# The written order of an attention and token-mixing kernel: later loads, stores and the steps behind the first scores rearranged

## Chip, cores and metric

The kernel runs on one core of one Trainium2 chip. The metric is device time in microseconds (us) of one execution. Five engines with a queue each take part: PE (matrix products; its weight loads are shown as PEld), DVE and ACT (elementwise work, and the only two that read PE's results here), POOL (elementwise work in on-chip memory, and the issue of DMAs that convert float32 to bfloat16) and SP (the issue of DMAs).

## The reference, cut to what matters

Per batch and head, 32 learned tokens p attend over the sequence, and the sequence then attends over the 32 packed tokens. A mixing layer over the tokens and an output projection follow.

```python
p_packed = sm_attn(p, k, v)              # scale, softmax over 576 keys
out = sm_attn(q, p_packed, p_packed)     # softmax over 32 packed tokens
x = out.transpose(0, 2, 1, 3).reshape(B, S, H * D)      # 8 x 576 x 512
wq, wk = x @ w_q, x @ w_k                               # 512 -> 64
mixed = einsum('bst,btd->bsd', scale * wq @ wk^T, x)
result = maximum(mixed, 0) @ w_out                      # 8 x 576 x 512
```

There are 8 batches, 8 heads, 576 positions and a head size of 64; q, k, v and the result are float32 in HBM.

## The kernel before, in words

The work is cut by batch (b = 0 to 7) and, within a batch, into steps. One string, ORDER (L12 to L57), lists some 520 items; the loop at L599 emits them one after the other, and each engine executes its own items strictly in that order. `@A`, `@V`, `@P`, `@S` name the engine (ACT, DVE, POOL, SP) where there is a choice, and `=4,5` names the PSUM banks (eight banks hold PE's results until an engine has copied them out). Nothing else decides the order: an item that waits holds back everything behind it on its engine, and nothing on the others.

The items of a batch, in the order of their data:

- **Loads.** LD.k, LD.v, LD.q (L154 to L182) are issued by POOL; LD.v is two DMAs, LD.q7 and LD.r7 are the two halves of batch 7's q, LD.O is the output weight `wout`. There are four buffers of each kind (NL, L8).
- **First attention.** KT (L255) transposes k on DVE; S1 (L263) makes the scores on PE; X1 (L287) their exponentials on ACT; TE (L295) transposes them on DVE; PV (L306) multiplies by v on PE, with a column of ones for the sum; RC and PP (L318, L321) divide, PT (L326) transposes, both on DVE. QK (L331) multiplies the packed tokens by w_k and w_q; QKE (L341) copies the result out of PSUM, and QD (L344) copies part of it on POOL.
- **Second attention.** QV (L351) transposes q on DVE; S2 (L362) makes scores on PE; X2 (L375) exponentials on ACT; RS and RR (L390, L396) row sums and reciprocals on DVE (HA, L385, adds halves on POOL first for batch 5); AM (L401) multiplies on POOL; AT (L409) transposes on PE and AE (L421) copies out. The last number is the piece of the sequence (TCH, L359): 0 and 1 are 256 rows each, 2 the last rows, 3 is 0 and 1 together, 4 all.
- **Mixing.** WKQ and WE (L433, L456), GM and GE (L461, L470), Y and YE (L473, L481): PE, then a copy. MX and MR (L488, L494) make the mixed rows, RL, RLF and RLR (L515 to L524) apply the maximum with 0.
- **Output.** OT (L527) and OH (L574) multiply by `wout`, four matmuls for 128 rows; OE, OEF and OEH (L545, L548, L580) copy the result out, ST, STF and STH (L555, L588, L583) store it. OT.b.4 covers the remaining rows of two batches; OEF.b.4 copies them to a tile `orem` of which there are two (L550), so that OEF.5.4 writes what ST.1.4 (L557 to L559) stores from, and OEF.7.4 what ST.3.4 stores from. The tile `o` has six buffers (NO).
- **WARM** (L610) are matmuls on a constant tile whose result nobody reads; WARM.6 covers 6 x 128 columns.

HOLD.v7 (L567) is a tiny DMA on SP that reads v7's buffer: it is issued once v7 has landed, and SP's stores stand behind it.

Of the kernel before, what the change touches and what calls it, by code (L numbers as in the profile page):

```python
# [17 lines left out]
AM.0.2@P WARM.6=7 AT.0.2=7 AE.0.2@A RS.0.0@V RR.0.0@V KT.1.2@V WARM.5=6 S1.1=2,3,0,1 X1.1.0@A AM.0.0@P
RS.0.1@V AT.0.0=6 RR.0.1@V AE.0.0@V TE.1.0@V QD.0@P WARM.2=4 WKQ.0.0=4,5 WKQ.0.2 X1.1.1@A TE.1.1@V AM.0.1@P
AT.0.1=7 LD.q2 PV.1.0=2,3 PV.1.1 WE.0.0@V RC.1@V AE.0.1@A WKQ.0.1 WE.0.1@A WARM.2=6 GM.0=6 LD.k3 PP.1.1@V  # L20
PP.1.0@V PT.1@V QV.1.2@V GE.0@A WARM.1=0 Y.0=0,1 YE.0@A QK.1=4 QKE.1@V WARM.1=7 S2.1.2=2,3 S2.1.1=6,7 X2.1.2@A
RS.1.2@V S2.1.0=0,1 X2.1.1@A LD.O MR.0=4,5 RR.1.2@V AM.1.2@P RLR.0@A KT.2.2@V MX.0.1=2,3 WARM.3=6 AT.1.2=6
X2.1.0@A QD.1@P WARM.1=7 S1.2=4,5,0,1 RL.0.1@A LD.v3 AE.1.2@A MX.0.0=2,3 X1.2.1@A RS.1.0@V RR.1.0@V RS.1.1@V
AM.1.0@P X1.2.0@A TE.2.1@V RR.1.1@V AM.1.1@P TE.2.0@V RL.0.0@A WARM.6=7 AT.1.0=7 AE.1.0@V PV.2.0=0,1 PV.2.1
LD.k4 RC.2@V PP.2.0@V AT.1.1=6 AE.1.1@A LD.q3 LD.v4 WKQ.1.0=4,5 WKQ.1.2 WE.1.0@A PP.2.1@V WKQ.1.1 WE.1.1@A
PT.2@V QK.2=2 QKE.2@A QV.2.2@V LD.q4 WARM.1=3 GM.1=3 QD.2@P GE.1@A WARM.1=7 Y.1=6,7 S2.2.2=0,1 X2.2.2@A
KT.3.2@V S2.2.3=4,5 YE.1@A WARM.1=2 MX.1.0=2,3 X2.2.3@A MX.1.1=0,1 MR.1=6,7 RLR.1@A RS.2.4@V RL.1.0@A RR.2.4@V
# [1 line left out]
AM.2.3@P OT.0.3 OT.0.0=4,5 AT.2.3=2 TE.3.0@V PV.3.0=0,1 PV.3.1 OE.0.1@V LD.k5 OT.0.1 RC.3@V PP.3.1@V PP.3.0@V
AE.2.3@A LD.v5 WKQ.2.0=6,7 WKQ.2.1 LD.k6 OE.0.0@A PT.3@V LD.q5 WKQ.2.2 KT.4.2@V QK.3=3 WE.2.2@A QKE.3@A  # L30
OT.1.0=0,1 S1.4=4,5,6,7 X1.4.1@A QV.3.2@V GM.2=2 GE.2@A OT.1.1 OE.1.0@V X1.4.0@A TE.4.0@V Y.2=6,7 YE.2@A
S2.3.2=2,3 X2.3.2@A S2.3.3=4,5 MX.2.1=6,7 MX.2.0=2,3 OT.1.2=0,1 TE.4.1@V X2.3.3@A QD.3@P OT.1.3 RS.3.4@V
MR.2=4,5 RR.3.4@V AM.3.3@P AM.3.2@P RL.2.1@A RLR.2@V LD.v6 PV.4.0=6,7 RL.2.0@A PV.4.1 LD.q6 RC.4@V PP.4.1@V
OE.1.1@A PP.4.0@V PT.4@V OT.2.2=2,3 QK.4=4 QV.4.2@V AT.3.3=5 QKE.4@A AT.3.2=4 AE.3.2@A S2.4.2=0,1 X2.4.2@A
AE.3.3@V KT.5.2@V S2.4.3=6,7 X2.4.3@A RS.4.4@V WKQ.3.0=4,5 WKQ.3.2 WKQ.3.1 WE.3.2@A RR.4.4@V AM.4.3@P
S1.5=0,1,6,7 OT.2.3 X1.5.0@A AM.4.2@P X1.5.1@A TE.5.0@V QD.4@P GM.3=4 OT.2.0=0,1 TE.5.1@V LD.k7 GE.3@A Y.3=6,7
OE.2.1@A YE.3@A PV.5.0=4,5 PV.5.1 RC.5@V PP.5.0@V LD.v7 MX.3.0=2,3 RL.3.0@A MX.3.1=6,7 OT.2.1 OE.2.0@A
PP.5.1@V RL.3.1@V AT.4.2=4 PT.5@V LD.q7 AT.4.3=5 LD.r7 AE.4.2@A AE.4.3@A OT.3.0=2,3 KT.6.2@V HOLD.v7 MR.3=6,7
RLR.3@A OT.3.1 OE.3.0@A QV.5.2@V WKQ.4.0=0,1 WKQ.4.1 WKQ.4.2 WE.4.2@V S1.6=4,5,6,7 X1.6.0@A TE.6.0@V X1.6.1@A
TE.6.1@V OT.3.4=2 OEF.3.4@V GM.4=3 GE.4@A S2.5.2=0,1 ST.0.0@P X2.5.2@A S2.5.3=4,5 X2.5.3@A Y.4=6,7 YE.4@V  # L40
PV.6.0=0,1 PV.6.1 MR.4=2,3 RC.6@V PP.6.1@V PP.6.0@V PT.6@V ST.1.4 MX.4.0=6,7 RLR.4@A ST.0.1 MX.4.1=4,5
OT.3.2=2,3 OT.3.3 QV.6.2@V RL.4.0@A RL.4.1@A OE.3.1@A QK.5=1 QKE.5@A QK.6=0 QKE.6@A HA.5@P RS.5.4@V RR.5.4@V
S2.6.2=6,7 X2.6.2@A KT.7.2@V ST.1.1@P S2.6.3=4,5 X2.6.3@A RS.6.4@V OT.4.0=2,3 OT.4.1 S1.7=0,1,6,7 OE.4.0@A
AM.5.3@P AM.5.2@P AT.5.3=4 AT.5.2=5 AE.5.3@A OT.4.2=2,3 X1.7.1@A AE.5.2@V QD.5@P X1.7.0@A ST.2.0 WKQ.5.0=4,5
WKQ.5.1 WKQ.5.2 OT.4.3 WE.5.2@A RR.6.4@V AM.6.3@V AT.6.3=6 QV.7.1@V GM.5=7 AM.6.2@P TE.7.0@V AT.6.2=0 OE.4.1@A
TE.7.1@V PV.7.0=4,5 PV.7.1 AE.6.3@V GE.5@A Y.5=2,3 AE.6.2@A QV.7.0@V QD.6@P WKQ.6.0=6,7 RC.7@V WKQ.6.1
ST.3.1@P PP.7.0@V PP.7.1@V PT.7@V YE.5@A WKQ.6.2 WE.6.2@A ST.1.0 MR.5=0,1 RLR.5@V MX.5.0=2,3 RL.5.0@A
# [601 lines left out]
```

## Time and profile before

| what | value |
|---|---|
| median of 3 runs | 104.31 us (104.2 to 104.42) |
| the profiled execution | 105.18 us, of which 103.4 us are the span from the first to the last instruction or transfer |
| granted PE clock | 1.00 |
| HBM read, written | 30.15 MB, 9.44 MB |

The page gives busy time by engine, then the span in 40 slices of 2.585 us each, in which a digit is the busy share in tenths and GB/s is what the DMA engines wrote (a load that turns float32 to bfloat16 counts with its bfloat16 bytes, and reads twice as many). "Landing" is the time from the issue of a DMA to its completion. In rows of the timeline the columns are start, duration, engine, line, operation, tiles, shapes, count, and in brackets the engine's idle time before it with what ended it.

### The profile page before, as it was taken

The page shows a single profiled execution, that of the slowest core. Times are in us where ns is not written, and L with a number is a line of the kernel's source. Part 1 is how long each engine was busy: PE and PEld are TensorE (multiplying, and loading weights), DVE is VectorE, ACT ScalarE, POOL GpSimd, SP SyncE. Part 2 cuts the span into 40 slices and gives each one's busy share as a digit, 9 for nine tenths or more (in the row PEclk, how much of TensorE's full clock was granted, in tenths as well). Part 3 has the DMA queues.
Part 4 walks back from the last instruction along what each step waited for, and adds up shares of the span by engine and source line. Part 5 has one row for each costly group of instructions (what it writes and reads, how often), then busy time and mean ns, then how long its engine had stood idle before and what let it go on. Part 6 is the DMA issues. An engine that isn't in the chain of part 4 may idle for free.

```text
span 103.4 us, 3594 instructions
## 1 busy us (share of the span) xinstructions
PE 93.2 (90%) x1531; PEld 57.3 (55%) x1546; DVE 74.0 (72%) x139; ACT 65.2 (63%) x112; POOL 53.2 (51%) x83
## 2 busy tenths in 40 slices
...
DMA  1999999999999999999999999999999999965994
GB/s 27 233 229 207 213 210 206 210 213 209 209 213 209 207 209 211 213 210 209 213 208 210 216 207 206 213 210 210 208 314 406 413 422 403 410 266 227 388 361 163
DMA packets 13632, 25.13 MB, mean 243 GB/s; under 512 B 1073, under 2 KB 6449, under 8 KB 13617
## 3 DMA queue, kind: packets, MB, share of 16 engines
...
HBM read 30.15 MB, written 9.44 MB: 383 GB/s over the span
## 4 chain that ended last, share of the span: by engine, by line
PE 54%; DMA 22%; DVE 6%; ACT 6%; POOL 5%; issue 2%; SPq 1%; ACTq 0%; DVEq 0%; POOLq 0%
PE ps L540 27%; DMA k_sb<-in_k_dram 14%; DMA o<-in_moe_w_q_dram 8%; PE ps L315 4%; PE ps L373 3%; PE ps L419 3%; PE ps L446 3%; DVE kT L237 3%; ACT e L378 2%; PE ps L492 2%; PE ps L467 2%; PE ps L441 2%; POOL a L405 2%; PE ps L615 2%; PE ps L282 2%
## 5 line engine op out<-in xcount | busy, mean ns | idle before, releaser
L405 POOL TENSOR_TENSOR a<-e,rr 128x256 bf16<-128x256 f32 (+2 forms) x18 | 19.6, 1098 | 24.1 <-DVE rr L399 16.9
L540 PE MATMUL ps<-wout,relu 128*128 128x512 bf16 x112 | 29.2, 380 | 1.0 <-issue 0.5
L615 PE MATMUL ps<-o 128*128 128x128 f32 (+3 forms) x86 | 22.2, 397 | 1.3 <-DVE o L135 1.2
L540 PEld LDWEIGHTS <-relu 128*128 128x128 bf16 x124 | 10.6, 98 | 12.0 <-issue 1.8
L615 PEld LDWEIGHTS ps<-o 128*128 128x128 f32 x86 | 13.2, 213 | 6.0 <-issue 3.9
L128 ACT ACTIVATE o<-ps 128x1024 f32<-128x1024 f32 (+1 forms) x13 | 12.5, 959 | 4.2 <-PE ps L540 3.9
L293 ACT ACTIVATE e1T<-ps 128x576 bf16<-128x576 f32 x16 | 9.7, 653 | 7.2 <-PE ps L282 7.2
L394 DVE TENSOR_REDUCE rs<-e 128x16 f32<-128x512 f32 (+2 forms) x13 | 11.0, 850 | 2.9 <-ACT e L378 2.8
L378 ACT ACTIVATE e<-ps 128x256 f32<-128x256 f32 (+2 forms) x19 | 11.3, 625 | 2.3 <-PE ps L373 2.2
L237 DVE STREAM_TRANSPOSE kT<-k_sb 128x1152 uint32<-128x1152 uint32 (+1 forms) x9 | 11.0, 1218 | 2.1 <-DMA k_sb<-in_k_dram 2.1
L503 ACT ACTIVATE relu<-ps 128x1024 bf16<-128x1024 f32 (+1 forms) x12 | 11.1, 957 | 1.3 <-PE ps L492 1.2
L237 DVE STREAM_TRANSPOSE qT<-q_sb 128x1152 uint32<-128x1152 uint32 (+1 forms) x10 | 11.0, 1108 | 0.7 <-DMA q_sb<-in_q_dram 0.7
L173 POOL DMA_DIRECT2D v_sb<-in_v_dram x16 | 10.2, 648 | 0.3 <-POOL v_sb L206 0.3
L128 ACT ACTIVATE aT<-ps 128x128 bf16<-128x128 f32 (+2 forms) x12 | 6.4, 548 | 5.8 <-PE ps L419 4.4
L237 DVE STREAM_TRANSPOSE e<-e1T 128x288 uint32<-128x288 uint32 x16 | 7.1, 458 | 1.6 <-ACT e1T L293 1.3
L315 PE MATMUL ps<-v_sb,e 64*64 64x192 bf16 x288 | 7.5, 245 | 0.0
L128 ACT ACTIVATE wkq<-ps 128x448 bf16<-128x448 f32 (+1 forms) x8 | 5.8, 728 | 2.3 <-PE ps L446 1.4
L132 DVE COPY o<-ps 128x512 f32<-128x512 f32 (+2 forms) x7 | 5.4, 768 | 2.6 <-PE ps L540 1.9
L446 PE MATMUL ps<-aT,pqk 128*128 128x256 bf16 (+1 forms) x48 | 6.8, 246 | 0.0
L315 PEld LDWEIGHTS <-e 64*64 64x64 bf16 x288 | 5.9, 107 | 1.3 <-DVE e L237 0.9
L373 PE MATMUL ps<-ppT,qT 64*128 64x64 bf16 x320 | 6.5, 190 | 0.0
L441 PE MATMUL ps<-pqk,aT 128*128 128x64 bf16 x80 | 6.2, 194 | 0.3 <-ACT aT L128 0.2
...
## 6 DMA issues: line engine op xcount, KB each, us to landing
v_sb<-in_v_dram POOLq DMA_DIRECT2D x16, 288.0 KB, 11.2
out_dram<-o SPq DMA_DIRECT2D x8, 512.0 KB, 6.5
k_sb<-in_k_dram POOLq DMA_DIRECT2D x7, 576.0 KB, 12.9
q_sb<-in_q_dram POOLq DMA_DIRECT2D x6, 576.0 KB, 13.3
out_dram<-o POOLq DMA_DIRECT2D x5, 512.0 KB, 9.1
out_dram<-o SPq DMA_DIRECT2D x5, 256.0 KB, 2.4
q_sb<-in_q_dram POOLq DMA_DIRECT2D x4, 288.0 KB, 11.3
out_dram<-orem SPq DMA_DIRECT2D x4, 256.0 KB, 6.1
```

Of the source, the lines that this page charges most:

```text
L128: nc.scalar.activation(o, i, COPY)
L173: nc.gpsimd.dma_start(v_bufs[b % NL][halves(i), 0:7:2], src)
L237: nc.vector.transpose(o, i)
L293: nc.scalar.activation(e1T[:, x], T["s1", b][x].rearrange("a c m -> a m c"), EXP, scale=scale)
L315: nc.tensor.matmul(T["pv", b][halves(cc), i], lhsT, rhs, start=n == 0, stop=n == R - 1, skip_group_check=True)
L378: nc.scalar.activation(e2[:, t0:t1].rearrange("a t (i y n) -> a y (t i) n", i=2, y=2), T["s2", b, c].rearrange("a y t i n -> a y (t i) n") ...
L394: nc.vector.tensor_reduce(rs[:, t0 * H:t1 * H], src, axis=AX, op=ADD)
L405: e.tensor_tensor(a2[:, t0:t1].rearrange("a t i (u l) -> a (t i u) l", l=L), e2v(b, c), T["rr", b][:, t0 * H:t1 * H].to_broadcast((P, (t1 ...
L446: nc.tensor.matmul(o, pqk[:, i, Dl:], aT[:, i, c0:c1], start=i == 0, stop=i == 1)
L503: nc.scalar.activation(o, i, RELU)
L540: nc.tensor.matmul(ps, lhsT, wout[:, j, :], start=j == 0, stop=j == NJ - 1)
L615: nc.tensor.matmul(bank(int(bk), [w]), warm[:, 0:P], rhs, start=True, stop=True)
```

## The change

Only ORDER is edited. The items are the same apart from the WARM items (74 units of 128 columns before, 69 after). What moves:

- **Start.** NC.0 goes from ACT to DVE; SET.v3 goes ahead of SET.mask, WC.1 ahead of WC.0, and both ahead of SET.v1 and SET.v2; LD.k2 is issued ahead of LD.v1.
- **Loads.** POOL issues k2 v1 q1 v2 q2 O k3 v3 k4 q3 v4 q4 k5 v5 q5 k6 v6 q6 k7 v7 q7 r7 behind k1, where it issued v1 q1 k2 v2 q2 k3 O v3 k4 q3 v4 q4 k5 v5 k6 q5 v6 q6 k7 v7 q7 r7. LD.q7 and LD.r7 now stand behind ST.3.4, QD.5 and HA.5 on POOL.
- **Behind the first scores.** RS.0.1 and RR.0.1 go ahead of KT.1.2, and KT.2.2, S1.2, GM.0 and Y.0 ahead of PV.1; the output products begin with OT.0.0 behind GM.1, where they began with OT.1.4 behind S1.3.
- **Stores.** POOL issues ST.3.4, ST.1.1, ST.0.1, ST.3.0, ST.5.1 (before: ST.0.0, ST.1.1, ST.3.1, ST.4.1, ST.3.0), the second to fourth of them behind AM.5.2 and ahead of AM.6.2. Behind HOLD.v7, SP issues ST.2.1, ST.1.4, ST.4.0, ST.2.0, ST.0.0, ST.3.1, ST.5.4 and so on (before: ST.1.4, ST.0.1, ST.2.0, ST.1.0, ST.5.4).
- **The end.** OT.5.4 goes ahead of S2.7; in batch 7, MR.7, MX.7.0, MX.7.1 are followed by OT.7.4 and OT.7.1 (before: MX.7.1, MX.7.0, MR.7, OT.6.3, OT.7.4, OT.7.2).
- **Copies.** 43 copies or elementwise steps change between ACT and DVE, 22 to ACT and 21 to DVE.

The diff, cut to the lines of which the prediction speaks:

```diff
-LD.g0 LD.v0 LD.r0 LD.q0 LD.k1 NC.1@A PX.1@V NC.0@A PX.0@V SET.aff@P SET.idb@V KT.0.0@V KT.0.1@V SET.mask@P
...
-S1.3=4,5,6,7 X1.3.1@A X1.3.0@A TE.3.1@V OT.1.4=2 OT.0.2=6,7 OEF.1.4@A RL.1.1@V AM.2.2@P AT.2.2=3 AE.2.2@V
...
-S2.7.0=4,5 MX.5.1=0,1 RL.5.1@V OT.5.4=6 GM.6=7 GE.6@V X2.7.0@A OEF.5.4@A ST.5.4 ST.4.1@P S2.7.2=2,3 X2.7.2@A
-S2.7.1=4,5 X2.7.1@A ST.3.0@P QK.7=0 RS.7.0@V RS.7.2@V RR.7.0@V AM.7.0@P Y.6=6,7 ST.2.1 YE.6@A OT.5.0=2,3
...
-YE.7@V OE.6.0@A OT.6.2=4,5 MX.7.1=6,7 RLF.7.1.1@A OEF.6.2@V MX.7.0=2,3 MR.7=0,1 RLR.7@V ST.5.1 OT.6.3 STF.6.2
-OT.7.4=4 RLF.7.0.0@V RLF.7.1.0@A RLF.7.0.1@V OT.7.2=0 OEF.7.2@V OEF.6.3@A ST.6.0 STF.6.3 OT.7.0=5 OEF.7.0@V
...
+LD.g0 LD.v0 LD.r0 LD.q0 LD.k1 NC.0@V PX.0@V NC.1@A PX.1@V SET.aff@P SET.idb@V SET.v3@P KT.0.0@V SET.mask@P
+WC.1@P WC.0@P LD.k2 SET.v1@P LD.v1 SET.v2@P KT.0.1@V WARM.4=0 WARM.22.128=0 S1.0=0,1,2,3 X1.0.1@A TE.0.1@V
...
+WE.1.0@V S2.2.2=6,7 WE.1.1@A X2.2.2@A S2.2.3=4,5 X2.2.3@A GM.1=1 OT.0.0=2,3 GE.1@V Y.1=6,7 OT.0.1 YE.1@A
...
+AT.4.2=1 AE.4.2@A OEF.3.4@A QV.5.2@V AT.4.3=5 AE.4.3@V ST.3.4@P QK.5=4 QKE.5@V QD.5@P S2.5.2=2,3
...
+OE.4.0@A ST.1.1@P WKQ.5.1 RS.6.4@V WE.5.2@A RR.6.4@V ST.4.0 ST.0.1@P S1.7=2,3,6,7 X1.7.1@A AM.6.3@V ST.3.0@P
...
+PT.7@V MR.5=0,1 RLR.5@A MX.5.1=6,7 RL.5.1@A MX.5.0=4,5 RL.5.0@V WKQ.6.0=0,1 WKQ.6.1 WKQ.6.2 WE.6.2@A OT.5.4=2
+OEF.5.4@A S2.7.1=6,7 ST.5.4 ST.1.0 GM.6=3 GE.6@V X2.7.1@A RS.7.1@V RR.7.1@V S2.7.2=0,1 X2.7.2@A S2.7.0=4,5
+QK.7=2 X2.7.0@A RS.7.0@V RR.7.0@V Y.6=6,7 YE.6@A OT.5.2=0,1 MX.6.1=4,5 QKE.7@A MX.6.0=6,7 AM.7.1@P RS.7.2@V
...
+ST.6.0 STF.6.3 YE.7@A ST.5.0 MR.7=6,7 RLR.7@A MX.7.0=4,5 RLF.7.0.1@A RLF.7.0.0@V MX.7.1=2,3 RLF.7.1.0@A
+OT.7.4=0 OEF.7.4@A ST.7.4 RLF.7.1.1@V OT.7.1=6 OEF.7.1@V OT.7.0=7 STF.7.1 OT.7.2=1 OEF.7.0@A OH.7.0=0 STF.7.0
```

More of the change, by code (lines that the diff above doesn't have):

```diff
@@ L13 @@
 LD.N0@A LD.N1@S SET.warm@V SET.v0@V SET.aT0@V SET.aT1@V SET.aT2@V SET.idf@V LD.W0@A LD.W1@S SET.tab@A LD.h0
-LD.g0 LD.v0 LD.r0 LD.q0 LD.k1 NC.1@A PX.1@V NC.0@A PX.0@V SET.aff@P SET.idb@V KT.0.0@V KT.0.1@V SET.mask@P
-WARM.4=0 WARM.22.128=0 S1.0=0,1,2,3 X1.0.1@A TE.0.1@V X1.0.0@A TE.0.0@V SET.v2@P WARM.8=4 PV.0.0=4,5 PV.0.1
-RC.0@V PP.0.0@V PP.0.1@V PT.0@V WC.0@P QV.0.0@V WC.1@P WARM.6=6 QK.0=6 SET.v3@P QV.0.1@V QKE.0@A WARM.4=7
-S2.0.2=2,3 X2.0.2@A RS.0.2@V RR.0.2@V SET.v1@P S2.0.0=0,1 X2.0.0@A LD.v1 LD.q1 LD.k2 S2.0.1=4,5 X2.0.1@A LD.v2
@@ L18 @@
[L18 to L27, printed above, removed]
@@ L28 @@
-S1.3=4,5,6,7 X1.3.1@A X1.3.0@A TE.3.1@V OT.1.4=2 OT.0.2=6,7 OEF.1.4@A RL.1.1@V AM.2.2@P AT.2.2=3 AE.2.2@V
[L29 to L47, printed above, removed]
@@ new lines @@
+X1.0.0@A TE.0.0@V WARM.8=4 PV.0.0=4,5 PV.0.1 RC.0@V PP.0.0@V PP.0.1@V LD.q1 PT.0@V WARM.6=6 QK.0=6 QKE.0@A
+QV.0.0@V QV.0.1@V QD.0@P WARM.4=7 S2.0.2=2,3 X2.0.2@A RS.0.2@V RR.0.2@V S2.0.0=0,1 LD.v2 S2.0.1=4,5 X2.0.0@A
+RS.0.0@V RR.0.0@V X2.0.1@A RS.0.1@V RR.0.1@V AM.0.2@P WARM.6=7 AT.0.2=7 AE.0.2@A AM.0.0@P WARM.5=6 AT.0.0=6
+KT.1.2@V AM.0.1@P WARM.3=2 AT.0.1=7 AE.0.1@A AE.0.0@V WKQ.0.0=2,3 WKQ.0.2 WE.0.0@A LD.q2 WKQ.0.1 KT.2.2@V
+S1.1=0,1,4,5 WE.0.1@A GM.0=6 X1.1.0@A TE.1.0@V GE.0@A WARM.2=7 Y.0=2,3 YE.0@V S1.2=0,1,6,7 MR.0=2,3 X1.1.1@A
```

33 lines of the change are left out of this document (28 added, 5 removed).

## The prediction

> **What bounds the kernel now.** I read the page's engine row and its slices first, then PE's busy time by stage, then the chain of work that ended last.
>
> ```profile
> PE 93.2 (90%) x1531; PEld 57.3 (55%) x1546; DVE 74.0 (72%) x139; ACT 65.2 (63%) x112; POOL 53.2 (51%) x83
> DMA  1999999999999999999999999999999999965994
> GB/s 27 233 229 207 213 210 206 210 213 209 209 213 209 207 209 211 213 210 209 213 208 210 216 207 206 213 210 210 208 314 406 413 422 403 410 266 227 388 361 163
> ```
>
> Two resources are full. The DMA engines are busy from the second slice to about 90 us. PE is busy for 90% of the span, but not all of that is work:
>
> ```profile
> 14.97:38.80 23.83, 22.04 (x441) 13.90 (x441) 18.80 (x36) 14.58 (x30) 13.54 (x20) 1.00 1.16 210
> 38.80:84.90 46.10, 43.76 (x861) 26.98 (x874) 40.54 (x67) 37.21 (x61) 25.43 (x32) 1.00 1.12 248
> 84.90:99.20 14.30, 14.14 (x110) 7.17 (x112) 7.84 (x17) 9.43 (x17) 2.86 (x4) 1.00 0.88 345
> ```
> ```profile
> 9.00:38.80 29.80, 14.37 (x43) 6.44 (x41) 1.00 1.16 210
> ```
>
> The first fence gives stages (length, then PE, PEld, DVE, ACT, POOL busy), the second the WARM line L615 alone. Up to 38.8 us nearly half of PE's time is WARM: PE waits there for loads. From 38.8 us it has no WARM left, and idles 46.10 - 43.76 = 2.34 us in the middle and 0.16 us in the last stage. So the end is set by when PE gets enough work, and by every stall behind that. The chain says the same: one load, then PE.
>
> ```profile
> 13.49 14.35 DMA k_sb<-in_k_dram
> 94.26 3.78 PE ps L540 x17
> 99.16 0.42 DVE o L132
> ```
>
> The load is LD.k2: issued at 13.49, landed at 27.84. After PE come copies on DVE and the last stores.
>
> **The change part by part.**
>
> *Start.* Moving NC.0 and the memsets is worth 0, since the second half of k0 is late in either order (KT.0.1 waits for it), and S1.0 needs KT.0.1. If that cover went, 0.6 us of NC.0 would show.
>
> ```profile
> 9.47 0.78 DVE L237 STREAM_TRANSPOSE kT<-k_sb 128x576 uint32<-128x576 uint32 x1 [1.20 <-DMA k_sb<-in_k_dram]
> ```
>
> *Loads and the first output products.* The stream is full, so places in it are exchanged, not gained. k2 takes v1's place, q1 takes k2's (27.8 us), and `wout` goes ahead of k3:
>
> ```profile
> 22.62 0.73 POOL L176 DMA_DIRECT2D k_sb<-in_k_dram  x1
> 23.34 0.78 POOL L166 DMA_DIRECT2D wout<-in_moe_w_out_dram  x1
> wout<-in_moe_w_out_dram POOLq DMA_DIRECT2D x1, 512.0 KB, 15.4
> PEld L540 <- DMA wout<-in_moe_w_out_dram: 0.5, 1, 0.5
> ```
> ```profile
> k_sb<-in_k_dram POOLq DMA_DIRECT2D x1, 576.0 KB, 12.9
> ```
>
> k3 lands at 22.62 + 12.9 = 35.5, `wout` at 23.34 + 15.4 = 38.7, and PE's first weight load for L540 waits for it. Exchanged, `wout` lands near 35.9 and k3 near 38.6. The other condition for OT.0.0 is that GM.1 in front of it is through. In before, QV.1.2 ends at 25.79 and GM.1 starts at 34.80:
>
> ```profile
> 24.45 1.34 DVE L237 STREAM_TRANSPOSE qT<-q_sb 128x1152 uint32<-128x1152 uint32 x1
> 27.86 1.38 DVE L237 STREAM_TRANSPOSE kT<-k_sb 128x1152 uint32<-128x1152 uint32 x1 [0.56 <-DMA k_sb<-in_k_dram]
> 34.80 0.46 PE L467 MATMUL ps<-wkq,a 128*128 128x64 bf16 x10
> 36.94 0.61 PE L492 MATMUL ps<-wkq,y 64*128 64x512 bf16 x4
> 37.82 0.75 PE L282 MATMUL ps<-kT,pT 32*32 32x288 bf16 x32 [0.22 <-ACT e L378]
> 39.01 0.81 PE L540 MATMUL ps<-wout,rem 128*128 128x512 bf16 x2 [0.45 <-ACT relu L503]
> ```
>
> Those 9.0 us hold KT.2.2 (1.38) and its wait (0.56), which have left this stretch for an earlier one: about 7.1 remain. QV.1.2 now ends at 27.85 + 1.34 = 29.2, so GM.1 starts near 36.2 and OT.0.0 near 36.4, where before the first output product starts at 39.01. What before had done by 39.01 and after has not: Y.1 (0.2), MX.1 and MR.1 (0.7 up to their overlap), S1.3 (0.4 to 0.75), together 1.3. The lead is 39.0 - 36.4 - 1.3 = **1.3 us**. Bounds: 0 (q1 or `wout` later by 1.3) and 2.6 (all of the earlier start). The WARM items between AT.1.0 and there, four in before, are gone in after; they cost nothing while PE waits anyway. The granted clock is 1.00 in every stage above, so no row shows what open gaps would do to it: 0 taken, up to 1 us lost, part of rival 2.
>
> *The middle.* PE's work from here is the same, and I followed both ACT and DVE through it with the durations of before. I find stalls of the same kind as the 2.34 us of before (OT.2.0 waits until ACT has done both RL.2.0 and RL.2.1, PV.6 waits for TE.6.1). The exchanged copies are 22 to ACT and 21 to DVE. I take 0, bounds -1.2 and +1.2, half of the stall either way. On POOL, a DMA starts only when the one eight before it has landed:
>
> ```profile
> 35.82 0.71 POOL L182 DMA_DIRECT2D q_sb<-in_q_dram  x1 [0.77 <-DMA k_sb<-in_k_dram]
> 47.45 0.71 POOL L182 DMA_DIRECT2D q_sb<-in_q_dram  x1 [2.35 <-DMA q_sb<-in_q_dram]
> ```
>
> (q4 starts when k3 is in, q5 when q3 is.) LD.v7 now stands ahead of AM.4.3; its second half waits for v5 and ends about when RR.4.4 is ready, so AM.4.3 loses nothing, or up to 1 us if v5 is late. LD.q7 and LD.r7 stand behind HA.5 and ST.3.4, two or three us later than before, but k7 and v7 are still ahead of them in the stream: 0.
>
> *The stores, and the wait that they add.* OEF.5.4 overwrites the tile from which ST.1.4 stores, so it waits for that landing. In before it starts on ACT at 83.90:
>
> ```profile
> 83.90 0.62 ACT L128 ACTIVATE orem<-ps 128x512 f32<-128x512 f32 x1
> 64.97 0.59 POOL L179 DMA_DIRECT2D q_sb<-in_q_dram  x1
> q_sb<-in_q_dram POOLq DMA_DIRECT2D x1, 288.0 KB, 12.8
> 65.50 0.61 POOL L561 DMA_DIRECT2D out_dram<-o  x1
> out_dram<-o POOLq DMA_DIRECT2D x1, 512.0 KB, 13.5
> 71.20 0.63 POOL L561 DMA_DIRECT2D out_dram<-o  x1
> out_dram<-o POOLq DMA_DIRECT2D x1, 512.0 KB, 10.4
> 74.93 0.60 SPq L572 DMA_DIRECT2D touch<-v_sb  x1
> touch<-v_sb SPq DMA_DIRECT2D x1, 0.1 KB, 6.2
> 75.58 0.59 SPq L559 DMA_DIRECT2D out_dram<-orem  x1
> out_dram<-orem SPq DMA_DIRECT2D x1, 256.0 KB, 6.5
> 76.21 0.64 SPq L561 DMA_DIRECT2D out_dram<-o  x1
> out_dram<-o SPq DMA_DIRECT2D x1, 512.0 KB, 7.1
> ```
>
> Adding issue and landing: the last load is in at 77.8, POOL's two stores at 79.0 and 81.6, SP's tiny HOLD at 81.1, ST.1.4 at 82.1 (1.8 us ahead of OEF.5.4), ST.0.1 at 83.3. HOLD carries 0.1 KB and takes 6.2 us: SP's transfers come out behind what POOL had queued. In after, POOL has queued by then ST.3.4 (256 KB) ahead of q7, and **three** stores of 512 KB instead of two; and on SP, ST.2.1 (512 KB) stands ahead of ST.1.4. From 77.8: ST.3.4 0.6, three stores at 1.3 (the first one's price) 3.9, ST.2.1 1.2 (83.3 - 82.1), ST.1.4 0.5 to 0.9: ST.1.4 lands at 84.2. Upper end: POOL's stores at (81.6 - 77.8)/2 = 1.9 each give 86.0. Lower end: SP's 768 KB take turns with POOL's from 78.4 on, at half rate, 2 x 1.7: 81.8. I take 84.2, nearest to what the tiny HOLD shows.
>
> OEF.5.4 would be due at 82.3 (83.90 less the lead of 1.3, and OT.5.4 now ahead of S2.7). The wait is 84.2 - 82.3 = **1.9 us**. Behind it on ACT stand X2.7.1, X2.7.2, X2.7.0, YE.6 and QKE.7; on PE, QK.7 needs the bank that OEF.5.4 empties, Y.6 the banks that X2.7.1 empties, OT.5.2 those of X2.7.2. So PE cannot run ahead, and everything behind it is later by the whole wait. Bounds: 0 and 3.7.
>
> [...]
>
> *The tail.* Behind QK.7 and Y.6 both orders have the same PE work. In before OT.6.3 and OT.7.4 cover the last RLF copies; in after OT.7.4 alone stands between MX.7.1 and OT.7.1, which needs all four:
>
> ```profile
> 94.72 1.28 DVE L505 TENSOR_SCALAR relu<-ps 128x512 bf16<-128x512 f32 x2
> 95.07 1.03 PE L540 MATMUL ps<-wout,rem 128*128 128x512 bf16 x4
> 97.72 2.17 SPq L590 DMA_DIRECT2D out_dram<-o  x3
> ```
>
> Two RLF copies in a row on DVE take 1.28 us and begin 0.2 behind MX.7.1, OT.7.4 covers 0.9 of that (1.03 less its overlap with the next product): 0.6, less the 0.16 us that PE idles there in before: + **0.45**, bounds 0 and 0.9. The last two copies go to two engines instead of one, but SP still issues the last stores one behind the other (2.17 for three): 0, bounds -0.4 and 0.
>
> *Sum:* -1.3 + 0 + 1.9 + 0.45 = +1.05 us on the span, 103.4 to 104.45. The profiled execution took 105.18, that is 1.78 around the span and 0.87 over the median; I add the difference to the median: 104.31 + 1.05 = **105.4 us**.
>
> **The rivals.**
>
> 1. *SP's stores take turns with POOL's, and ST.1.4 lands in time* (the faster side). Then -1.3 + 0.45 = -0.85: 103.5 us. For: POOL's second store took 2.6 us behind its first (81.6 - 79.0), double the first's 1.3, so something shared the engines with it. Against: HOLD's 6.2 us. It decides from the point where the wait is under 0.85, that is ST.1.4 landing before 83.15. Chance 0.24.
> 2. *The lead is lost in the early or middle part* and OEF.5.4 is due late, so that the wait is hidden: + 0.45 to +1.5 of new stalls: 104.8 to 105.8 us. For: many small waits are exchanged and each can only be followed roughly. Chance 0.12.
> 3. *The stores bound the end.* The 9.44 MB of the table at some 410 GB/s (the page's row) are 23 us behind the last load at 77.8, so a span under about 102 isn't to be had. This only cuts off gains; it is a part of rival 1.
> 4. *Nothing moves:* lead and losses cancel within 0.2 us. Chance 0.08.
>
> **How the numbers follow.** The forecast (lead, wait, tail) has 0.56. It spreads from 104.5 (landing at 83.3) to 107.2 (86.0). The range takes in rival 1 and most of that: 103.4 to 107.0; forecast's own range 104.6 to 107. About 0.2% is what a measurement of this kernel can tell from no change: faster by more 0.24, slower by more 0.67 (forecast and rival 2, less their edges), within 0.09.
>
> **What would show it.** Right: output products from about 36.4 us; ACT idle for over 1 us ahead of its `orem` row near 84 us with a store as the releaser; PE idle near 83 to 85 us. Wrong: no idle time there (rival 1), or a first output product at 38 us or later (rival 2). Also wrong: POOL's loads not back to back between 58 and 70 us, which would move q7.

## The result, and the profile after

| kernel | median | lowest to highest | ratio to before, 95% interval |
|---|---|---|---|
| before, on the same chip | 104.42 us | 104.2 to 105.04 | 1 |
| changed | 108.34 us | 106.91 to 108.98 | 1.0295 (1.0239 to 1.0351) |

The change costs 3.9 us. I had forecast +1.05 us and 105.4 us, with 107.0 as the upper end: the direction was right, and the time lies above the range. Ratios, here and below, leave out executions over 1.5% slower than the fastest of the same kernel, so where a kernel's times scatter the ratio is lower than the quotient of the medians. The profiled execution took 107.26 us, with a span of 105.5 us.

Lines of the changed kernel are one lower than those of before (L539 for L540); those of most experiments are two lower. The changed kernel's page, in the order of the lines shown of before:

```profile
PE 93.9 (89%) x1536; PEld 55.7 (53%) x1536; DVE 73.9 (70%) x140; ACT 65.1 (62%) x111; POOL 53.1 (50%) x83
DMA  2999999999999999999999999999999999663894
GB/s 26 230 222 212 214 217 206 205 213 207 210 207 210 209 211 212 211 209 212 217 201 213 212 205 211 212 208 234 240 373 403 417 410 414 279 244 151 317 369 158
```

The totals hardly differ. The stages do: the changed kernel's windows from the first packed QK to the first output product, to S1.5, to the end of S2.7, to QK.7, and to PE's end (length, then PE, PEld, DVE, ACT and POOL busy, granted clock, DMA share, GB/s):

```profile
14.72:35.98 21.26, 18.90 (x388) 11.67 (x388) 16.29 (x34) 12.40 (x26) 13.53 (x21) 1.00 1.15 210
35.98:57.57 21.59, 20.60 (x364) 11.01 (x361) 17.96 (x29) 16.58 (x26) 12.54 (x17) 1.00 1.15 210
57.57:83.75 26.18, 25.61 (x542) 15.62 (x543) 23.04 (x40) 22.12 (x36) 13.24 (x17) 1.00 1.11 267
83.75:85.91 2.16, 0.00 (x0) 0.03 (x1) 0.00 (x0) 0.65 (x2) 0.00 (x0) 1.00 1.03 417
85.91:101.60 15.69, 15.51 (x124) 7.80 (x123) 9.61 (x17) 9.69 (x19) 3.52 (x5) 1.00 0.75 298
```

The fourth row is new: 2.16 us in which PE and DVE do nothing at all, while the DMA engines are full. The timeline of PE in the changed kernel, at the first output product and at that gap:

```profile
35.85 1.03 PE L539 MATMUL ps<-wout,relu 128*128 128x512 bf16 x4
...
83.21 0.54 PE L372 MATMUL ps<-ppT,qT 64*128 64x64 bf16 x24
85.91 0.41 PE L335 MATMUL ps<-wqk,ppT 64*64 64x128 bf16 x8 [2.16 <-ACT orem L127]
```

and ACT's:

```profile
81.70 0.92 ACT L127 ACTIVATE wkq<-ps 128x896 bf16<-128x896 f32 x1
85.27 0.60 ACT L127 ACTIVATE orem<-ps 128x512 f32<-128x512 f32 x1 [2.64 <-DMA out_dram<-orem]
```

ACT is through with WE.6.2 at 82.62 and stands 2.64 us ahead of OEF.5.4, until ST.1.4 has landed. All three marks that I had set are there: an output product near 36.4 us, ACT idle with a store as the releaser, PE idle near 83 to 85. When the transfers landed, from issues and their landing times (POOL's three stores, SP's touch, ST.2.1 and ST.1.4, and the last load):

```profile
out_dram<-o POOLq DMA_DIRECT2D x1, 512.0 KB, 8.6
out_dram<-o POOLq DMA_DIRECT2D x1, 512.0 KB, 10.2
out_dram<-o POOLq DMA_DIRECT2D x1, 512.0 KB, 11.5
touch<-v_sb SPq DMA_DIRECT2D x1, 0.1 KB, 6.1
out_dram<-o SPq DMA_DIRECT2D x1, 512.0 KB, 7.7
out_dram<-orem SPq DMA_DIRECT2D x1, 256.0 KB, 8.9
q_sb<-in_q_dram POOLq DMA_DIRECT2D x1, 288.0 KB, 10.7
```

They were issued at 72.18, 72.85, 73.45, 74.99, 75.64, 76.31 and 67.69, so they landed at 80.8, 83.1, 85.0, 81.1, 83.3, 85.2 and 78.4. SP's transfers came in between POOL's, each 0.2 to 0.3 us behind one of them; my sum had ST.2.1 and ST.1.4 behind all three. ST.1.4 needed 2.4 us more than its issue in before did (6.5).

### The profile page after: what moved, and what is told of

It reads as the page before. It is cut to its first block, busy times and chain, and to the rows that moved or that the text cites. A ratio compares the mean times of both kernels' runs of the same rounds, so it can differ in the third digit from the quotient of the medians.

```text
span 105.5 us, 3595 instructions
## 1 busy us (share of the span) xinstructions
PE 93.9 (89%) x1536; PEld 55.7 (53%) x1536; DVE 73.9 (70%) x140; ACT 65.1 (62%) x111; POOL 53.1 (50%) x83
## 4 chain that ended last, share of the span: by engine, by line
DMA 59%; PE 15%; POOL 8%; DVE 5%; issue 4%; ACT 4%; SPq 2%; ACTq 0%; POOLq 0%; DVEq 0%
DMA v_sb<-in_v_dram 30%; DMA q_sb<-in_q_dram 12%; PE ps L539 10%; DMA out_dram<-orem 8%; DMA o<-in_moe_w_q_dram 8%; POOL a L404 3%; DVE rs L393 2%; ACT e L377 2%; POOL v_sb L172 2%; POOL k_sb L175 1%; DVE qT L236 1%; POOL v_sb L205 1%; PE ps L576 1%; DVE rr L398 1%; PE ps L418 1%
## 5 line engine op out<-in xcount | busy, mean ns | idle before, releaser
L539 PE MATMUL ps<-wout,relu 128*128 128x512 bf16 x124 | 30.7, 380 | 0.1
L614 PE MATMUL ps<-o 128*128 128x128 f32 (+3 forms) x76 | 20.2, 414 | 1.2 <-DVE o L134 1.2
L539 PEld LDWEIGHTS <-relu 128*128 128x128 bf16 x124 | 10.8, 98 | 11.8 <-issue 1.3
L614 PEld LDWEIGHTS ps<-o 128*128 128x128 f32 x76 | 12.0, 221 | 5.3 <-issue 3.6
L127 ACT ACTIVATE o<-ps 128x1024 f32<-128x1024 f32 (+2 forms) x13 | 11.4, 879 | 5.4 <-PE ps L539 5.2
L502 ACT ACTIVATE relu<-ps 128x1024 bf16<-128x1024 f32 (+1 forms) x14 | 13.0, 968 | 1.1 <-PE ps L491 1.1
L131 DVE COPY o<-ps 128x1024 f32<-128x1024 f32 (+2 forms) x7 | 6.6, 958 | 5.0 <-PE ps L539 2.7
L127 ACT ACTIVATE aT<-ps 128x128 bf16<-128x128 f32 (+2 forms) x11 | 5.0, 465 | 5.8 <-PE ps L418 3.5
L127 ACT ACTIVATE wkq<-ps 128x448 bf16<-128x448 f32 (+1 forms) x10 | 7.2, 730 | 1.8 <-PE ps L445 1.7
L372 PEld LDWEIGHTS <-qT 64*128 64x128 bf16 x320 | 5.4, 94 | 2.8 <-DVE qT L236 1.7
```

What stands on the lines that cost most here:

```text
L127: nc.scalar.activation(o, i, COPY)
L372: nc.tensor.matmul(ps[:, y, t - t0, i], lhsT, rhs, start=e == 0, stop=e == 1)
L502: nc.scalar.activation(o, i, RELU)
L539: nc.tensor.matmul(ps, lhsT, wout[:, j, :], start=j == 0, stop=j == NJ - 1)
L614: nc.tensor.matmul(bank(int(bk), [w]), warm[:, 0:P], rhs, start=True, stop=True)
```

## The experiments

My theory W: the wait for ST.1.4 costs the time, and PE's idleness in it may cost granted clock too. Rival C: the new order itself is slower, and the wait only shows it. Times are medians, ratios are to before on the same chip.

### Take the wait away: a third `orem`

```diff
-        a2 = new("a2", b, [P, 5, 2, P])
+        a2 = new("a2", b, [P, 5, 2, P], bufs=2)
-            copy(eng, new("orem", b // 2, [P, D], fp32, bufs=2), T["otf", b, t])
+            copy(eng, new("orem", b // 2, [P, D], fp32, bufs=3), T["otf", b, t])
```

> The changed order, with a third `orem` buffer, so that ScalarE's copy of batches 4 and 5 has no store to wait for; the masked products `a2` give up their third buffer to make room. Theory W (the wait of that copy for the landing of ST.1.4 costs about 2.6 us, and TensorE's 2.2 us idle in it also costs granted clock in some runs): the copy starts by 82.8 instead of 85.3, QK.7 follows S2.7 without a gap of over 0.3 us, the span is 102.6 to 103.0 (105.5 less 2.6), the clock is 0.99 or more in every run, and the median is 104.3 to 105.0, against about 108 for the changed kernel. Rival C (the new order itself loses the time, in its tail or by what it does to SP's and POOL's queues, and the wait only shows it): the copy starts early but the span stays above 104.5 and the median above 106.

Measured: 104.23 us, ratio 0.9995 (0.9972 to 1.0017), span 102.5. OEF.5.4 in this kernel, on ACT:

```profile
81.40 0.92 ACT L127 ACTIVATE wkq<-ps 128x896 bf16<-128x896 f32 x1
82.26 0.60 ACT L127 ACTIVATE orem<-ps 128x512 f32<-128x512 f32 x1
```

No idle time in front of it. The whole loss of the change, 4.1 us against 108.34 (on chips on which before differs by 0.13), hangs on this one wait; rival C falls. The edit also takes a buffer from `a2`; the run below in which POOL's stores are moved has no wait either, leaves `a2` alone and comes to the same ratio, 1.00. But the wait is 2.64 us long, so 1.5 us are still to be explained. And without its wait the changed order is no faster than before: the lead of 1.3 us that I had forecast is missing.

### Move the store, two ways

First ST.1.4 ahead of ST.2.1 on SP:

```diff
-RL.4.1@A QK.6=4 QKE.6@A QV.6.2@V ST.2.1 S2.6.2=6,7 X2.6.2@A S2.6.3=2,3 ST.1.4 MR.4=4,5 X2.6.3@A
+RL.4.1@A QK.6=4 QKE.6@A QV.6.2@V ST.1.4 ST.2.1 S2.6.2=6,7 X2.6.2@A S2.6.3=2,3 MR.4=4,5 X2.6.3@A
```

> The changed order with one item moved: ST.1.4 stands ahead of ST.2.1 on SP. Theory W with stores of SP served in the order of issue: ST.1.4 is issued at about 75.6 and lands at about 82.3 to 83.3 (as ST.2.1 did), the copy starts at 82.6 to 83.4, the gap of TensorE ahead of QK.7 falls from 2.2 to under 0.8 us, the span is 102.7 to 103.6 and the median 104.4 to 105.4. Rival R (stores take turns on the DMA engines, so that the place in the queue hardly counts): ST.1.4 still lands at about 85, and the span stays at 105 to 105.5, the median above 106.5.

Measured: 104.79 us, ratio 1.005 (1.0027 to 1.0072). ACT's row in this kernel:

```profile
82.80 0.60 ACT L126 ACTIVATE orem<-ps 128x512 f32<-128x512 f32 x1 [0.82 <-DMA out_dram<-orem]
```

The wait fell from 2.64 to 0.82 us: the place on SP counts. Then the other queue: ST.1.4 stays behind ST.2.1, but POOL's ST.0.1 and ST.3.0 go behind QD.6:

```diff
-ST.0.1@P S1.7=2,3,6,7 X1.7.1@A AM.6.3@V ST.3.0@P
+S1.7=2,3,6,7 X1.7.1@A AM.6.3@V
...
-AE.6.2@A QD.6@P PV.7.1
+AE.6.2@A QD.6@P ST.0.1@P ST.3.0@P PV.7.1
```

> The changed order, with POOL's stores ST.0.1 and ST.3.0 moved behind QD.6, from about 72.9 and 73.5 to about 80 us. Rival T (the stores of the two queues share the DMA engines, so that POOL's stores in flight hold ST.1.4 back by half of their own time each or more): ST.1.4 lands at 82.7 to 84.0 instead of 85.2, ScalarE's copy waits 0.2 to 1.4 us instead of 2.6, median 104.6 to 106.0. Rival O (SP's stores are held back by those ahead of them on SP alone): ST.1.4 lands at 84.9 to 85.4, the wait stays above 2.2 us, and the median above 106.8.

Measured: 104.57 us, ratio 1.0003 (0.9977 to 1.0028). The landing of ST.1.4, issued at 77.04, and the copy:

```profile
out_dram<-orem SPq DMA_DIRECT2D x1, 256.0 KB, 5.2
```
```profile
82.39 0.60 ACT L126 ACTIVATE orem<-ps 128x512 f32<-128x512 f32 x1
```

It landed at 82.2, some 3 us earlier than in the changed kernel although it was issued 0.7 later; either expectation had it later. Two stores of 512 KB on another queue had held it back. With the landings shown above, SP's between POOL's, this fits the mechanism of my rival 1 (stores of the two queues take turns). But turns did not make ST.1.4 early: the touch, first on SP, landed only at 81.1 and the rest behind it, and no run here shows what holds the touch. One of the twelve executions took 105.64 us at a clock of 0.984; no trace shows it, so the reason is open.

### Put the wait into before

The order of before with ST.1.4 third on SP:

```diff
-PT.6@V ST.1.4 MX.4.0=6,7 RLR.4@A ST.0.1 MX.4.1=4,5
+PT.6@V MX.4.0=6,7 RLR.4@A ST.0.1 MX.4.1=4,5
...
-X1.7.0@A ST.2.0 WKQ.5.0=4,5
+X1.7.0@A ST.2.0 ST.1.4 WKQ.5.0=4,5
```

> The order of before with one item moved: ST.1.4 stands behind ST.0.1 and ST.2.0 on SP, so third instead of first after the touch. Theory W: two stores of 512 KB go ahead of it, at 1.2 us each alone and up to 2.3 beside POOL's, so it lands at about 85.5 instead of 82.1; the copy OEF.5.4, due at 83.0 to 83.9, waits 1.6 to 2.5 us, and the median is 105.9 to 107.0 with the clock at 1.00 (ratio 1.015 to 1.026), up to 108 if the clock falls as well. Rival N (a late store is absorbed, since DVE or TensorE have other work at that point in this order): under 104.9.

Measured: 109.8 us, ratio 1.0441 (1.039 to 1.0492), dearer than either number expected. The trace, of an execution of 110.68 us with a clock of 0.969, has both reasons (four of the six executions had 0.984, one 0.961). PE's timeline, then the clock by stretches (the number behind POOL's):

```profile
87.72 0.32 PE L475 MATMUL ps<-pp,g 64*64 64x128 bf16 x4 [3.30 <-ACT orem L126]
```
```profile
84.00:86.00 2.00, 0.41 (x13) 0.30 (x9) 0.59 (x1) 0.00 (x0) 0.00 (x0) 1.00 1.00 397
86.00:88.00 2.00, 0.28 (x5) 0.17 (x5) 0.03 (x1) 0.93 (x3) 0.00 (x0) 0.57 0.58 236
88.00:90.00 2.00, 1.78 (x12) 0.62 (x12) 1.50 (x5) 0.98 (x3) 1.30 (x2) 0.50 0.79 303
90.00:92.00 2.00, 2.00 (x11) 0.46 (x6) 1.22 (x1) 1.35 (x2) 1.56 (x3) 0.50 1.02 401
92.00:94.00 2.00, 2.00 (x12) 0.96 (x11) 0.00 (x0) 1.08 (x2) 0.00 (x0) 0.73 0.30 115
```

ST.1.4 landed at 87.0, not 85.5, and PE idled 3.30 us. Then PE ran at half clock until past 93 us. In the prediction I had set this cost to nothing.

### The clock: fill the gap and leave the wait

The changed order with filler in PE's idle stretch:

```diff
-S2.7.0=4,5 QK.7=2 X2.7.0@A
+S2.7.0=4,5 WARM.8=3 QK.7=2 X2.7.0@A
```

> The changed order, with filler matmuls of 3 x 128 columns x 4 quarters (`WARM.8=3`, about 0.5 to 2 us, on a bank that is free there and whose result nobody reads) ahead of QK.7, in TensorE's idle stretch at 84 to 86 us. The wait stays. Theory K (part of the change's loss is granted clock, lost because TensorE idles 2.2 us there): the clock is 0.995 or more in every timed run and the median is 106.8 to 107.3, against 108.3 of the changed kernel, whose runs had 0.984 in three of five. Rival Z (the lower clock comes by chance, not from that idle stretch): runs of 0.984 remain, with a median above 107.8.

Measured: 107.19 us, ratio 1.0241 (1.0212 to 1.0271), spans 105.0 to 105.6, clocks 0.992 to 1.000. The 0.992 is under the 0.995 that I had asked for; in its trace the clock is 1.00 up to 102 us, and 0.74 in the mean from there on, when PE has no work left. Work that nobody needs made the kernel 1.1 us faster. ACT still waits:

```profile
85.33 0.60 ACT L126 ACTIVATE orem<-ps 128x512 f32<-128x512 f32 x1 [2.71 <-DMA out_dram<-orem]
```

The changed kernel once more, for its clock:

> The changed kernel once more, for more runs of its clock and another trace. Theory K (the idle stretch of 2.2 us ahead of QK.7 is near the length from which the clock falls, so that it falls in a part of the executions): runs of two kinds, with spans of 105.0 to 105.6 us at 0.995 or more and of 106.3 to 107.3 us at 0.984. If the trace taken is of the second kind, its clock is 0.50 for about 3.4 us shortly behind 86 us and 1.00 before. Rival: the same clock in all runs.

Measured: 108.27 us, ratio 1.0275 (1.0189 to 1.0361). With the first series there are nine executions. Three ran at 0.997 to 1.000: 106.67, 106.91, 107.26 us. Six ran at 0.982 to 0.984: 107.84 to 108.98. The mean of the six is 108.54 and that of the three 106.95, 1.6 us apart. The trace taken here was one of the six. Its PE timeline, and the clock by the us:

```profile
86.08 0.41 PE L335 MATMUL ps<-wqk,ppT 64*64 64x128 bf16 x8 [2.19 <-ACT orem L127]
...
86.85 1.66 PE L539 MATMUL ps<-wout,relu 128*128 128x512 bf16 x4
```
```profile
86.00:87.00 1.00, 0.82 (x13) 0.57 (x13) 0.45 (x1) 1.00 (x4) 0.00 (x0) 1.00 0.98 387
87.00:88.00 1.00, 1.00 (x4) 0.26 (x2) 0.90 (x3) 0.84 (x3) 0.26 (x1) 0.55 1.01 404
88.00:89.00 1.00, 1.00 (x6) 0.29 (x6) 0.86 (x4) 0.00 (x0) 1.00 (x2) 0.50 1.05 418
89.00:90.00 1.00, 1.00 (x10) 0.37 (x5) 0.31 (x2) 0.86 (x1) 1.00 (x2) 0.50 1.02 410
90.00:91.00 1.00, 1.00 (x5) 0.41 (x4) 1.00 (x2) 0.17 (x1) 0.60 (x2) 0.74 0.76 307
```

The same idle stretch as in the first trace, 2.19 against 2.16 us. Here it is followed by some 3.4 us at half clock (the shares lost, 0.45 + 0.50 + 0.50 + 0.26, are 1.7 us, twice that at 0.50); in the first series a mean clock of 0.984 over a span of 106.5 us gives the same. Four matmuls of 512 columns took 1.66 us there, against 1.03 at the first output product.

The same filler in the injected wait, in the order of before:

```diff
-RR.7.0@V AM.7.0@P Y.6=6,7
+RR.7.0@V AM.7.0@P WARM.12=1 Y.6=6,7
```

> The order of before with ST.1.4 third on SP (109.8 us), and filler matmuls (`WARM.12=1`, 12 x 128 columns, some 3 us, result not read) in TensorE's idle stretch ahead of Y.6. The wait for the store stays. Theory K (in that run the idle stretch of 3.3 us lost clock: 0.50 from about 87 to 93 us, two thirds of the added time): clock 0.99 or more in every run, and the median falls by 2.5 to 3.5, to 106.3 to 107.3 us, that is before plus the bare wait. Rival Z (the lower clock is not set by that idle stretch): the median stays above 108.5 with clocks of 0.984 or less.

Measured: 107.55 us, ratio 1.0293 (1.0256 to 1.0329), clock 1.00 in all runs. 2.25 us came back, 0.25 less than expected at least. PE's rows in it:

```profile
84.59 2.84 PE L613 MATMUL ps<-o 128*128 128x512 f32 x6
87.36 0.25 PE L475 MATMUL ps<-pp,g 64*64 64x128 bf16 x4
```

PE goes on with Y.6 at 87.36, against 87.72 in the trace without the filler, so by these two traces some 0.4 of the 2.25 is a shorter gap, and some 1.9 goes with the clock. The wait itself was not the same in both: ACT's copy began at 85.69 here, 1.4 us earlier, and Y.6 then waited for the filler, which was too long.

### Where the lead went: halves and thirds

The early half alone, that is the changed order up to AM.3.2, and then the order of before to the end. Against the changed kernel:

```diff
 PV.4.1 RS.3.4@V RR.3.4@V LD.v6 AM.3.3@P AM.3.2@P
-RC.4@V OT.2.0=2,3 OT.2.1 LD.q6 OE.2.0@A PP.4.0@V
+LD.q6 RC.4@V PP.4.1@V PP.4.0@V PT.4@V OT.2.2=2,3
...
```

> The changed order up to and with AM.3.2 and the copy OE.1.1, then the order of before: the early output products alone, with the loads, stores and end of before. Theory W: the lead is kept to the end, 0.5 to 1.0 us; ST.1.4 lands at about 82, as before, and is due at about 83.0, so that there is no wait: span 102.4 to 102.9, clock 0.99 or more in all runs, median 103.4 to 104.0 against 104.4 of before: 0.990 to 0.998 of it. Rival E (the stores become the limit: the same landings as before, with work that is earlier, give a new wait at that copy or the one after): the copy waits 0.3 to 1 us and the span is 103.2 to 103.8. Rival C2 (the early order loses time in the middle): the span is above 103.8.

Measured: 104.91 us, ratio 1.0057 (1.0031 to 1.0083). There is no wait at the copy (span 103.0), and the early half still loses 0.6 us. W's gain did not come, nor rival E's new wait, nor a span as long as that of C2. A second trace of before bears on why my lead was not there:

> The kernel before once more, for a second trace. The one that I predicted from took 105.18 us, 0.87 above its median. Theory V (that execution lost most of this ahead of 32 us by late first loads, so that its stages all lay about 1 us too late against any changed kernel): here PV.0.0 starts at 11.8 to 12.3 us instead of 12.63, k2 lands at 26.5 to 27.3 instead of 27.84, S1.5 starts at 56.5 to 57.1 instead of 57.68, and the span is 102.2 to 102.9. Rival: the same times as in the first trace within 0.3 us up to 57 us, and the difference lies behind.

Measured: 104.53 us, span 102.7. PE's rows in it for PV.0.0, S1.5 and Y.6:

```profile
12.42 0.94 PE L315 MATMUL ps<-v_sb,e 64*64 64x192 bf16 x36
...
57.00 0.48 PE L282 MATMUL ps<-kT,pT 32*32 32x288 bf16 x32 [0.28 <-DVE kT L237]
...
83.91 0.24 PE L477 MATMUL ps<-pp,g 64*64 64x128 bf16 x2
```

PV.0.0 is 0.1 behind what theory V asked for, the rest as expected. The execution from which I predicted had reached S1.5 at 57.68, 0.68 later. So I compared an order walked through on paper with an execution that had lost most of its 0.87 us over the median ahead of S1.5. The same three marks and the span of all that bear on it:

| kernel | PV.0.0 | S1.5 | Y.6 | span |
|---|---|---|---|---|
| before, first trace | 12.63 | 57.68 | 84.57 | 103.4 |
| before, second trace | 12.42 | 57.00 | 83.91 | 102.7 |
| early half alone | 11.77 | 57.04 | 83.97 | 103.0 |
| changed, third `orem` | 11.94 | 57.26 | 83.46 | 102.5 |
| changed, POOL's stores later | 12.24 | 57.37 | 83.57 | 102.6 |
| changed, first trace | 12.31 | 57.57 | 86.40 | 105.5 |

Over eight traces with the early order of before S1.5 starts at 56.67 to 57.68, mean 57.15; over seven with the changed early order at 56.91 to 57.72, mean 57.35. The lead is -0.2 us, well inside that scatter, that is none. From S1.5 to Y.6 the late order of before takes 26.9, the changed one without its wait 26.2, and with it 28.83: a gain of 0.7, and a wait of 2.6. From Y.6 to the end before takes 18.8 and the changed order 19.0.

The gain of 0.7 goes with one output product: between S1.5 and Y.6 the two orders have the same items on PE, except that before has OT.2.0 and OT.2.1 there and the changed order OT.2.2 alone. Ahead of S1.5 the late order of before has OT.2.2, the changed one OT.2.0 and OT.2.1. Before's second trace, then the third-`orem` kernel, from S1.5 to Y.6:

```profile
57.00:83.91 26.91, 26.77 (x550) 16.43 (x552) 23.86 (x41) 24.04 (x39) 14.88 (x19) 1.00 1.11 267
```
```profile
57.26:83.46 26.20, 24.98 (x539) 15.63 (x549) 23.11 (x41) 23.25 (x39) 12.98 (x16) 1.00 1.11 268
```

In before PE is full there, 26.77 of 26.91 us, so most of a product (some 1.0 us) done ahead of S1.5 is gained. Ahead of S1.5 PE is not what sets the time: S1.5 waits for KT.5.2 on DVE (0.28 in the row of before above), and earlier output products only change where PE idles.

The first third alone, with the exchanged loads but without the early output products. Against the changed kernel:

```diff
 AM.1.1@P LD.k4 PP.2.0@V AE.1.2@A
-PP.2.1@V PT.2@V QK.2=4 AE.1.0@A QKE.2@A
+AE.1.0@V AT.1.1=6 AE.1.1@A LD.q3 LD.v4 WKQ.1.0=4,5
...
```

> The changed order up to and with AE.1.2, then AE.1.0 and the order of before: the exchanged loads k2, v1, q1 and the steps behind the first scores, without the early output products and without the other loads. The early half as a whole took 104.91 us, 0.6 above before. Theory M (it loses in the middle, where output products stand ahead of S2.3 and the chain from there over ScalarE, VectorE and GpSimd to the transposes of batch 3 runs later): 104.0 to 104.5 us here, the same as before. Rival F (it loses in the first 30 us, by v1 and q1 landing later): 104.7 to 105.2.

Measured: 106.67 us, ratio 1.02 (1.0167 to 1.0233). Both expected times were wrong; the loss is 2 us and lies early. DVE's wait for k3 and PE's S1.3 in it, then S1.3 in before's second trace:

```profile
37.93 1.38 DVE L235 STREAM_TRANSPOSE kT<-k_sb 128x1152 uint32<-128x1152 uint32 x1 [2.98 <-DMA k_sb<-in_k_dram]
```
```profile
39.37 0.48 PE L280 MATMUL ps<-kT,pT 32*32 32x288 bf16 x32 [1.14 <-DVE kT L235]
```
```profile
37.15 0.75 PE L282 MATMUL ps<-kT,pT 32*32 32x288 bf16 x32 [0.22 <-ACT e L378]
```

With `wout` ahead of it, k3 comes at 37.9, and S1.3 is 2.2 us later. Part of that is rival F's reason: GM.1 is 1.3 us later already (35.43 against 34.13), behind the later q1. So the exchange of loads loses 2 us, and the early output products, which fill that time, win most of it back (104.91 with them, though those two runs differ in later loads as well). The early half as a whole is no gain.

### The late half, and a version that beats both

The order of before up to PV.4.1, then the changed one. Against before:

```diff
 PV.4.0=6,7 RL.2.0@A PV.4.1
-LD.q6 RC.4@V PP.4.1@V OE.1.1@A PP.4.0@V PT.4@V OT.2.2=2,3
+OE.1.1@A RC.4@V OT.2.0=2,3 OT.2.1 LD.q6 OE.2.0@A PP.4.0@V
...
```

> The order of before up to the second value product of batch 4, then the changed order: the loads, the stores and the end of the change without its early output products. Theory W: the early lead of about 0.8 us is not there, ST.1.4 still lands at about 85 to 85.5 since its issue hangs on SP's order and the queue of POOL's transfers, and the landing sets the time of all that follows: span 105.2 to 105.8, the same as the whole change, the wait 1.7 to 2.4 us long, median 106.8 to 108.5. Rival L (the lead is gained and is kept, so that what is lost without it shows in full): 106.0 or more of span. Rival C (the late order is harmless, the early half does the harm): span 103.6 or less, median below 105.5.

Measured: 106.5 us, ratio 1.0218 (1.0193 to 1.0242), span 104.6. That is between the numbers of W and of rival C: the copy starts at 84.43, 0.1 behind the landing of ST.1.4, and in the trace PE idles 1.72 us ahead of S2.5.2 for the transpose of q5, which the runs below explain. With the third `orem` as well (the edit of the first experiment):

> The order of before up to the second value product of batch 4, then the changed order, and the third `orem` buffer (with `a2` down to two). Four kernels are timed so far: before 104.29 us, the changed order without its wait 104.23, the early half alone 104.91, the late half alone 106.5. Theory S (three terms that add: the early half costs 0.6 us, the late half without its wait gains 0.7, the wait costs the rest): 104.23 less 0.6, so 103.4 to 103.9 us, ratio 0.992 to 0.997 of before, span 101.7 to 102.1, clock 1.00. Rival G (the early half gains as I predicted, and its own timing above is an accident of the stores): 104.9 or more. Rival H (the halves need each other, so that neither gains alone): 104.1 to 104.5.

Measured: 105.63 us, ratio 1.0096 (1.007 to 1.0122). Theory S and rival H failed; the time is in the range of rival G (104.9 or more), but its reason, that the early half gains, isn't what the trace shows. The cause stands in DVE's timeline, and so does its cure:

```profile
63.18 1.38 DVE L235 STREAM_TRANSPOSE qT<-q_sb 128x1152 uint32<-128x1152 uint32 x1 [1.31 <-DMA q_sb<-in_q_dram]
```

The early half of before loads k6 ahead of q5; the late half of the change wants q5 earlier. So, the same kernel with the two exchanged:

```diff
-LD.k6 OE.0.0@A PT.3@V LD.q5
+LD.q5 LD.k6 OE.0.0@A PT.3@V
```

> The late half with the third `orem` buffer, as in the run of 105.63 us, with one item moved: LD.q5 stands ahead of LD.k6. In that run q5 landed at 63.16 us, and TensorE and VectorE waited for it between QK.5 (62.78) and S2.5.2 (64.62), where the changed order with the same third buffer has 62.92 and 63.33. Theory Q (that load alone cost 1.3 to 1.5 us, and the three terms do add): q5 lands at about 61, S2.5.2 follows at 62.8 to 63.2, span 101.8 to 102.6, median 103.5 to 104.2, ratio 0.990 to 0.997. Rival H (the halves fit only each other, so that the next load or step is late instead): above 104.4.

Measured: 104.57 us, ratio 0.9975 (0.9954 to 0.9997); S1.5 at 56.98, Y.6 at 83.26, span 102.3. S2.5.2 follows at 63.14 without a wait, and the time falls by 1.1 us, so the load was the cause of most of what the 105.63 lost, and rival G falls too. But 104.57 is above theory Q's 104.2, where I had put rival H, and so the three terms aren't shown to add: the trace, of an execution of 104.10 us, 0.47 under the median, does meet theory Q's marks. It also fits the reading of the output product: with OT.2.0 and OT.2.1 ahead of S1.5, S1.5 starts no later than in before's second trace (57.00), and Y.6 0.65 earlier. Last, with two `orem` buffers again and the stores in their better places:

```diff
-QV.6.2@V ST.2.1 S2.6.2=6,7 X2.6.2@A S2.6.3=2,3 ST.1.4
+QV.6.2@V ST.1.4 ST.2.1 S2.6.2=6,7 X2.6.2@A S2.6.3=2,3
-ST.0.1@P S1.7=2,3,6,7 X1.7.1@A AM.6.3@V ST.3.0@P
+S1.7=2,3,6,7 X1.7.1@A AM.6.3@V
-AE.6.2@A QD.6@P PV.7.1
+AE.6.2@A QD.6@P ST.0.1@P ST.3.0@P PV.7.1
```

> A version made of orders alone, with two `orem` buffers as in both kernels: the order of before up to the second value product of batch 4 with LD.q5 ahead of LD.k6, then the changed order with ST.1.4 ahead of ST.2.1 on SP and POOL's ST.0.1 and ST.3.0 behind QD.6. ST.1.4 should land at 81.3 to 82.3, the copy OEF.5.4 be due at 81.8 to 82.4 and wait at most 0.3 us. If theory Q holds: 103.5 to 104.3 us, below both kernels. If stores or q5 are late all the same: 104.5 to 105.5.

Measured: 104.17 us, ratio 0.9954 (0.9934 to 0.9975), clear of before, and 4 us under the changed kernel. The copy starts at 82.28 without a wait. This version keeps the late order, drops the early one, and has its stores placed so that the copy doesn't wait for them. By these runs the rearranged late order is worth 0.5%.

## Why the prediction was wrong, step by step

- **The wait of OEF.5.4.** Named in the right place, with the right followers, and mis-sized: 1.9 forecast, 2.64 measured. Due at 82.6 instead of 82.3, which is near by luck: there was no lead, but the late order had gained 0.7, and the first trace of before lay 0.7 late at this copy (83.90, where the second has 83.24). The landing was 85.2 instead of 84.2: of that 0.6 because the last load landed at 78.4 instead of 77.8, the rest the stores' own. The working behind it was wrong: I let all of POOL's three stores through ahead of SP's, and SP's came in between them.
- **The lead of 1.3 us.** This step failed. I counted PE's work ahead of a mark in the middle of a stretch in which PE isn't the limit (S1.5, at its end, waits for DVE), and took before's times from one execution that ran late. The first output product did come at 35.85 (36.4 forecast). At S1.5 nothing was left of it (-0.2).
- **The middle, 0 with bounds of 1.2.** It gained 0.7, with the one output product more that was put ahead of S1.5.
- **The tail, +0.45.** +0.2.
- **The clock, "0 taken, up to 1 us lost, part of rival 2".** This step failed as well. It is no matter of rival 2 but a part of the forecast itself, since the wait makes the gap. It costs 1.6 us in six of nine executions, and so all of it in the median.
- **Rival 2.** Its first half came true, the lead was lost; its second did not, since the late order's gain kept the copy from being due late, and the wait showed in full.
- **Rival 1.** Its mechanism fits (two of POOL's stores held ST.1.4 back some 3 us, and SP's landed between POOL's), its result did not come. No run shows the half rate from which I estimated its landing of 81.8: ST.1.4 landed at 85.2, and at 82.2 with two of POOL's stores moved. Turns alone don't account for the touch of 0.1 KB either, which took 6.1 us (6.2 in before).

Together: 0.2 - 0.7 + 2.64 + 0.2 = 2.3 us at full clock, on 104.42: 106.8 us, where the three executions at full clock have 106.95. With 1.6 us of clock it is 108.4, where the median was 108.34. What isn't explained is some 0.4 us of the early half's 0.6 (0.2 of it stands at S1.5), why the kernel with q5 moved gains only 0.25%, and why the touch takes 6 us.
